# Moving fold steps, one load and one small product between the slots of a hand-scheduled kernel (FFT mixing followed by a low-rank mixer, one core)

## The chip, the cores and the metric

The kernel runs on one core of a Trainium2 chip. A core has TensorE for matmuls (PE in the profile, PEld for its weight loads), VectorE (DVE), ScalarE (ACT), GpSimd (POOL), SyncE (SP), whose queue issues most transfers here, and 16 DMA engines. The metric is the time of one execution on the device, in microseconds; several runs are made and their median is the number that counts.

## The reference

`x` is 8 batches of 3136 rows of 256 channels, float32. Two things are computed one after the other:

```python
X = np.fft.fft(x, axis=1)              # along the 3136 rows
X = np.fft.fft(X, axis=2)              # along the 256 channels
x = X.real.astype(np.float32)

xt = x.transpose(0, 2, 1)
h = xt @ U @ V                         # rank 32 over the rows
u = x + h.transpose(0, 2, 1)
ch = np.maximum(u @ w_ch1, 0.0) @ w_ch2   # 256 -> 1024 -> 256
out = (u + ch).astype(np.float32)
```

## The kernel before

The work has two layers that run interleaved: a transform of each batch (the two Fourier transforms and the low-rank part), and a mixer over chunks of rows that yields the output.

**Transform of a batch b.** Rows of `x` are loaded into one buffer each: `xf` (rows in reversed order, by four gathers on POOL, line 57) and `xr` (rows in order, by two transfers on SP, line 76, and small ones for a single partition, lines 87 to 102). There is one `xf` and one `xr`, so a load of the next batch has to wait until the present batch's part has been read. `load_part` (line 487) loads half a batch. `fold` (line 471) yields the steps that turn them into the operands of the transform, by sums and differences on VectorE, all recorded through `fold_tt` (line 452, so that the profile has them under L453):

- `along_d` (line 416) adds or subtracts mirrored channels: `eof<-xf` and `eor<-xr`; `alone` (line 423) copies the two channels left over, on POOL.
- `mirror` (line 427) makes `eos` out of `eof` and `eor`; `half` and `fourth` make `ge`, `go` and `gc`.

For a batch after the first two the steps come in this order, counted from 0: `eof`, `eof`, `eor`, `eor`, load of the next batch's first half, `eos`, `eos`, `eof`, `eof`, `eor`, `eor`, load of the next batch's second half, `eos`, `eos`, `ge`, the two `gc`, `go`. Batch 1 has its `eor` steps in the part before the loop, and so four steps fewer: its step 7 is the load of batch 2's second half. The last batch loads nothing.

Then `transform` (line 928) gives the matmul steps: `even_rows` and `seq` (tiles `pt`, with `ev` and `eh` copied or made from them), `join` and `mirrored` (sums on VectorE into the tiles `A`, `B` and `tab`), the channel steps `chan` (line 656: two matmuls into `pst`, then a copy into `S` or `T`), `lowrank` (line 670: `ptt`, copied by ScalarE into `tl` and `ta`), and `hidden` (line 740: `pq` from `tl`, copied into `qt`), whose result is spread by a DMA transpose into `qf` (line 750). All PSUM tiles of the transform, and the tiles `ph` of the mixer, share two buffers, named `dft`.

**Mixer over chunks.** The 8 x 1568 rows of half the batches are cut into 25 chunks c of 512; each chunk also gives the mirrored rows of the other half (hf = 1). For each chunk and half, `front` (line 770) makes two small matmuls `ph` and sums them on VectorE with `S` and `T` into `u` (line 799, under L458); a DMA transpose on SP brings `u` into `ut` (line 813), of which POOL makes the small tiles `fx` (lines 816, 817). `odd_part` (line 820) makes `uo = S - T`. `direct` (line 829) multiplies `u` of the first half with W1 (`p<-u,w`), ScalarE applies relu into `h` (line 843); `mirrors` (line 845) corrects the same PSUM tiles to the other half by `uo` and `qf` (`p<-uo,wd`, `p<-dv,qf`), again with relu (line 859). `second_product` (line 890) multiplies `h` with W2 (`p<-w,h`, two PSUM buffers named `p2`), VectorE adds `ut` into the output tile `o` (lines 921, 922), POOL corrects a column by `fx` (line 926), and `store` (line 879) sends `o` out over SP. There are two buffers of `o`.

**Order.** Each chunk of the loop (line 1182) has slots: 0 to 5 and a few fractions between them. `turn(c, sl)` runs what is due in slot 6c + sl. The tuple `FOLDS` (line 1131) and the lists behind it (lines 1137 to 1139, counted from mid - 18, where mid is the batch's first transform slot) say in which slot each fold step of a batch is recorded; `transform` gives its steps from slot mid on. A slot 0 comes right after `direct(c, 0)` and `odd_part(c)`; slot 1 in the middle of a second product; slot 1.75 after `front(c, 1)`; 4.75 after `front(c + 1, 0)`; slot 5 after `second_product(c, 0, 0)`.

What is recorded is not yet the order on an engine: a scheduler places instructions when it thinks them ready. `keep_in_program_order`, which `fold_tt` and `mm` call, holds an instruction behind the one that was recorded just before it on its engine, and behind no other. An instruction without this hold, like `uo`, `u` and `o` in the later chunks or any DMA, can move.

Of the kernel before, what the change touches and what calls it, by code (L numbers as in the profile page):

```python
# [31 lines left out]
def kernel(  # L32
# [9 lines left out]
    nc = tc.nc  # L42
    B, S, D = x.shape
# [418 lines left out]
    def mm(*a, **k):  # L462
        ins = nc.tensor.matmul(*a, **k)  # L463
        if len(pinned) > 1:
            tc.keep_in_program_order(ins)
        if pinned:
            pinned.append(ins)
# [77 lines left out]
    def seq(b, par, typ, pn, tag="dft", part=True):  # L545

        d = state(b)
        ne = NE if b else 0
        pt = psum.tile([P, QW + NE], FP32, tag=tag, name="pt", bufs=BUFS[tag])
        d["pt"] = pt  # L550
        todo = products(b, par, typ, P * typ, pn == 1, ne)
        if typ == 0 and b == 0:
            todo = todo + products(b, par, 1, 256, (pn == 1) == (par == 1), ne)
        elif typ == 0 and pn == 1:
            todo = todo + [(QW, w, rhs) for w, rhs in u_odd(b, 1, 256)]
        add_up(pt, todo)
        if pn == 0:
            ev = d["ev"] = wp.tile([P, QW], FP32, tag="ev", name="ev", bufs=EB)
            w = (2 * NT if par else TE) + ne
            nc.scalar.copy(ev[:, :w], pt[:, :w])  # L560
            if part:
                apart(b, par)
# [12 lines left out]
    def join(b, par, typ, kept=None, low=True, high=True):  # L575

        d = kept or ST[b]
        ne = NE if b else 0
        pt, ev = d["pt"], d["ev"]
        dst = ST[b]["A"] if typ == 1 else ST[b]["B"]  # L580
        p_, e_ = pt[:, 0:2 * NT], d["eh"][:]
        up, dn = dst[:, 1176:784:-1], dst[:, 1177:HALF + 1]
        if low:
            nc.vector.tensor_tensor(up, p_, e_, op=AL.add)
        if not high:
            return
        if typ == 1:
            nc.vector.tensor_tensor(dn, e_, p_, op=AL.subtract)
        else:
            nc.vector.tensor_tensor(dn, p_, e_, op=AL.subtract)  # L590
        if ne:
            pu, eu = 2 * NT, NT
            nc.vector.tensor_tensor(ST[b]["tab"][:, typ, par, :].rearrange("p (g r) -> p g r", r=R),
                                    four(pt[:], pu), four(ev[:], eu), op=AL.add)
            if typ == 0:
                alt = dst[0:1, 786:HALF + 1:2]
                nc.vector.tensor_single_scalar(alt, alt, -1.0, op=AL.mult)
                nc.vector.tensor_copy(ST[b]["tab"][0:1, 0, 1, :].rearrange("p (g r) -> p g r", r=R),  # L598
                                      four(pt[0:1], QW))

    def even_rows(b, typ, pn, tag="dft"):

        d = state(b)
        ne = NE if b else 0
        if pn == 0:
            d["pe"] = psum.tile([P, QW], FP32, tag=tag, name="pt", bufs=BUFS[tag])
        pt = d["pe"]
        todo = products(b, 0, typ, P * typ, pn == 1, ne)
        if typ == 0:
            todo = todo + products(b, 0, 1, 256, pn == 0, ne)  # L610
        for n, (at, w, rhs) in enumerate(todo):
            mm(pt[:, at:at + rhs.shape[-1]], w, rhs, start=(pn == 0 and n == 0),
               stop=(n == len(todo) - 1), skip_group_check=True)
        if pn == 0:
            ev = d["ve"] = wp.tile([P, QW], FP32, tag="ev", name="ev", bufs=EB)
            nc.scalar.copy(ev[:, :TE + ne], pt[:, :TE + ne])  # L616
            return
        dst = d["A"] if typ == 1 else d["B"]
        nc.scalar.copy(strip(dst[:], 392, [[-2, NT + 1]]), pt[:, 0:NT + 1])
        nc.scalar.copy(strip(dst[:], 391, [[-2, NT]]), pt[:, NT + 1 + ne:TE + ne])  # L620
        if ne:
            nc.scalar.copy(d["tab"][:, typ, 0, :].rearrange("p (g r) -> p g r", r=R), four(pt[:], TE - NT))
# [7 lines left out]
    def mirrored(b, typ, kept):  # L630

        ne = NE if b else 0
        pt, ev = kept["pe"], kept["ve"]
        dst = ST[b]["A"] if typ == 1 else ST[b]["B"]
        nc.vector.scalar_tensor_tensor(strip(dst[:], 394, [[-1, 2], [2, NT]]),
                                       strip(ev[:], 1, [[NT + ne, 2], [1, NT]]), 2.0 if typ else -2.0,
                                       strip(pt[:], 1, [[NT + ne, 2], [1, NT]]),
                                       op0=AL.mult, op1=AL.subtract if typ else AL.add)
# [17 lines left out]
    def chan(b, ch, h, tag="dft", eng=None):  # L656
        d = ST[b]
        at, n0 = ((0, 0), (785, 1), (393, 786), (1177, 785))[ch]
        n = 393 if ch == 0 else 392
        if b == 0 and ch == 2:  # L660
            at, n0, n = 392, 784, 393
        pt = psum.tile([P, TE], FP32, tag=tag, name="pst", bufs=BUFS[tag])
        mm(pt[:, :n], MC[:, h * P:(h + 1) * P], d["A"][:, at:at + n], start=True, stop=False)
        mm(pt[:, :n], (MSX if ch == 3 and b == 0 else MSN)[:, h * P:(h + 1) * P], d["B"][:, at:at + n],
           start=False, stop=True)
        to = d["ST"[h]][:, n0:n0 + 2 * n - 1:2]
        eng = eng or (nc.vector.tensor_copy if b == 0 and h == 1 else nc.scalar.copy)
        eng(to, pt[:, :n])  # L668
# [71 lines left out]
    def hidden(b):  # L740

        pt = psum.tile([P, JT, R], FP32, tag="dft", name="pq", bufs=BUFS["dft"])
        for j in range(JT):
            for s in range(2):
                mm(pt[:, j, :], W1[:, s, j * P:(j + 1) * P], TL[:, s, :], start=(s == 0), stop=(s == 1))
        nc.scalar.copy(QT[:], pt[:].rearrange("p j r -> p (j r)"))
        if b > 1:
            spread_rank(b)

    def spread_rank(b):  # L750

        (nc.scalar if b == 1 else nc.sync).dma_start_transpose(out=QF[b % 2][:], in_=QT[:])
# [175 lines left out]
    def transform(b):  # L928

        def odd_rows(typ, pn):  # L930
            seq(b, 1, typ, pn)
            if pn:
                join(b, 1, typ)

        def even(typ, pn):
            even_rows(b, typ, pn)
            if pn:
                mirrored(b, typ, ST[b])

        a = [lambda pn=pn: even(1, pn) for pn in range(2)]  # L940
        s = [lambda pn=pn: even(0, pn) for pn in range(2)]
        c = [lambda pn=pn: odd_rows(1, pn) for pn in range(2)]
        d = [lambda pn=pn: odd_rows(0, pn) for pn in range(2)]
        rank = [lambda: lowrank(b)]
        ch = [lambda ch=ch, h=h: chan(b, ch, h) for ch in range(2) for h in range(2)]
        q = [lambda: hidden(b)]
        if b == 1:
            return 11, [a[:1], c[:1] + a[1:], c[1:] + d[:1], s[:1] + d[1:] + s[1:],
                        [lambda ch=ch: chan(b, ch, 0, eng=nc.vector.tensor_copy) for ch in (1, 0)], [ch[3], ch[1]],
                        rank + q + [lambda: spread_rank(b)]]  # L950
        if b == 2:
            return 23, [a[:1], a[1:] + c[:1], [], c[1:] + s[:1], s[1:], d[:1], d[1:], ch[:1], ch[1:2] + rank,
                        q, ch[2:3], ch[3:]]
        return 6 * (b * HALF // CH) - 15, [[x] for x in a + c + d[:1] + s + d[1:] + ch[:1] + rank + ch[1:2] + q + ch[2:]]
# [173 lines left out]
    def put(slot, *steps):  # L1128
        due.setdefault(slot, []).extend(steps)

    FOLDS = {1: (5, 5, 6, 6, 6, 7, 8, 8, 9, 9, 10, 10, 10.75),
             2: (13, 13.75, 15, 15, 15, 16, 16, 17, 18, 19, 20, 20, 20, 21, 21, 22, 22.75),
             3: (26, 26, 30, 30, 30, 31, 31, 32, 33, 33, 34, 34, 35, 35, 36, 37, 38)}
    for b in range(1, B):
        mid, steps = transform(b)
        todo = list(fold(b))
        places_ = FOLDS.get(b) or [mid - 18 + n for n in
                                   ((1, 2, 3, 5, 5, 5, 5, 8, 9, 10, 11, 11, 12, 13, 14, 15, 17) if b + 1 < B else
                                    (1, 2, 3, 5, 5, 5, 8, 9, 10, 11, 12, 13, 14, 15, 17))]
        assert len(todo) == len(places_)  # L1140
        for step, at in zip(todo, places_):
            put(at, step)
        for n, step in enumerate(steps):
            put(16.5 if mid + n == 17 and b == 1 else mid + n, *step)
# [98 lines left out]
```

## Time and profile before

| | |
|---|---|
| median of 3 runs | 440.24 us (439.96 to 440.59) |
| profiled execution | 440.81 us |
| its span in the profile | 439.0 us |
| granted TensorE clock, mean | 0.998 |
| DMA, mean over the span | 154 GB/s, 67.83 MB |

The profile lists instructions with their start and duration in microseconds from the start of the span; `x16` says that sixteen alike are merged in a row, and `[0.38 <-DVE u L458]` that the engine stood idle for 0.38 us before and what ended this. Tiles are written out<-in by the names above. Most matmuls are recorded by a helper and have L463. An engine with q behind its name (SPq) is its queue of instructions that issue DMAs. The ends of matmuls are modelled, so their starts are the better number. A matmul's record is missing here and there, so that a group of eight can show as x7.

### The profile page before, as it was taken

The numbers are of one execution on the slowest core, as the hardware profiler recorded it, in microseconds if no ns is written. First come the engines' busy times: TensorE is split into PE (matmuls) and PEld (weight loads), VectorE is DVE, ScalarE is ACT, GpSimd is POOL, SyncE is SP. The second block draws the span as 40 slices with busy tenths as digits, with TensorE's granted clock in tenths as the row PEclk, the third lists the DMA queues.
The fourth block names the chain that finished last, engine by engine and source line by source line (L and its number), as shares of the span: only waits on it lengthen the run. The fifth ranks groups of instructions, "written<-read, shape, count | busy, mean of one in ns | idle before, by whom it ended". The sixth has DMA issues, their size and how long they took to land.

```text
span 439.0 us, 9351 instructions
## 1 busy us (share of the span) xinstructions
PE 422.1 (96%) x3457; PEld 284.1 (65%) x3504; DVE 319.9 (73%) x665; ACT 292.2 (67%) x633; POOL 139.8 (32%) x340
## 2 busy tenths in 40 slices
PE   5989998999999999999999999999999999999996
PEld 2764675666666766666666766666666766666675
DVE  8988987987988887769867787679867554353442
ACT  7958764666667757766667757766667757765651
POOL 8971323452333235413343134231422100111111
PEclk9999999999999999999999999999999999999999
DMA  7897798959669685926776386676234423434543
GB/s 200 218 211 197 159 258 123 192 154 244 161 140 246 131 208 140 233 73 178 169 191 193 90 230 72 144 208 142 67 88 132 110 73 95 103 117 124 121 122 122
DMA packets 89165, 67.83 MB, mean 154 GB/s; under 512 B 55402, under 2 KB 82430, under 8 KB 89118
## 3 DMA queue, kind: packets, MB, share of 16 engines
q1 hardware_dynamic: 83350, 52.79, 49.7%
q0 software_dynamic: 5472, 14.36, 12.9%
q8 instruction: 27, 0.44, 0.4%
q14 instruction: 20, 0.16, 0.1%
q10 hardware_dynamic: 296, 0.07, 0.1%
HBM read 28.86 MB, written 25.69 MB: 124 GB/s over the span
## 4 chain that ended last, share of the span: by engine, by line
PE 87%; DVE 4%; ACT 3%; DMA 2%; POOL 2%; issue 1%; POOLq 0%; ACTq 0%
PE p L463 71%; PE pt L463 7%; PE pst L463 5%; PE ph L463 2%; DMA xf<-in_x_dram,xidx 2%; ACT h L843 1%; POOL xf L57 1%; DVE eof L453 1%; PE ptt L463 1%; DVE u L458 1%; PE pq L463 1%; DVE eor L453 1%; DVE eos L453 1%; ACT h L859 0%; POOL em L283 0%
## 5 line engine op out<-in xcount | busy, mean ns | idle before, releaser
L463 PE MATMUL p<-w,h 128*128 128x256 bf16 x1576 | 195.1, 273 | 0.0
L463 PEld LDWEIGHTS <-h 128*128 128x128 bf16 x1576 | 148.7, 98 | 39.8 <-issue 15.3
L859 ACT ACTIVATE h<-p 128x512 bf16<-128x512 f32 (+1 forms) x200 | 101.6, 593 | 82.8 <-PE p L463 79.3
L843 ACT ACTIVATE h<-p 128x512 bf16<-128x512 f32 (+1 forms) x200 | 101.7, 597 | 8.2 <-PE p L463 7.7
L926 POOL TENSOR_TENSOR o<-o,fx 128x2 f32<-128x2 f32 (+1 forms) x95 | 49.0, 516 | 155.4 <-DVE o L922 83.1
L463 PE MATMUL p<-u,w 128*128 128x512 bf16 (+1 forms) x354 | 90.8, 374 | 3.2 <-ACT u L723 0.5
L921 DVE TENSOR_TENSOR o<-p,ut 128x256 f32<-128x256 f32 (+1 forms) x95 | 39.6, 416 | 71.5 <-PE p L463 48.7
L463 PEld LDWEIGHTS <-w 128*128 128x128 bf16 x512 | 41.6, 97 | 38.4 <-issue 2.4
L463 PE MATMUL p<-uo,wd 128*128 128x512 bf16 (+1 forms) x199 | 50.6, 375 | 0.3
L458 DVE TENSOR_TENSOR u<-ph,T 128x512 bf16<-128x512 f32 (+23 forms) x63 | 34.3, 556 | 10.2 <-PE ph L463 8.1
L57 POOL DMA_INDIRECT xf<-in_x_dram,xidx x32 | 36.3, 1135 | 11.0 <-issue 6.8
L922 DVE TENSOR_TENSOR o<-p,ut 128x256 f32<-128x256 f32 (+1 forms) x95 | 38.8, 409 | 0.0
L453 DVE TENSOR_TENSOR eof<-xf 99x1016 bf16<-99x1016 f32 (+1 forms) x33 | 38.4, 1173 | 0.4 <-issue 0.4
L453 DVE TENSOR_TENSOR eor<-xr 99x1016 bf16<-99x1016 f32 (+1 forms) x34 | 38.6, 1146 | 0.0
L458 DVE TENSOR_TENSOR u<-ph,S 128x512 bf16<-128x512 f32 (+23 forms) x63 | 34.2, 554 | 0.8 <-PE ph L463 0.3
L817 POOL TENSOR_TENSOR fx<-ut 128x4 f32<-128x4 bf16 x48 | 17.7, 369 | 53.5 <-DMA ut<-u 53.4
L463 PEld LDWEIGHTS <-wd 128*128 128x128 bf16 x200 | 19.4, 98 | 13.1 <-issue 0.4
L463 PE MATMUL pt<-te,gc 98*128 98x229 bf16 (+1 forms) x192 | 24.0, 260 | 0.2 <-ACT ev L616 0.2
L668 ACT CAST T<-pst 128x392 bf16<-128x392 f32 (+1 forms) x28 | 17.1, 614 | 9.3 <-PE pst L463 9.3
L463 PE MATMUL pst<-A,mc 128*128 128x392 bf16 (+1 forms) x60 | 19.8, 330 | 3.2 <-DVE tab L598 1.6
L463 PEld LDWEIGHTS <-gc 98*128 98x128 bf16 x216 | 19.4, 97 | 4.3 <-issue 0.3
L668 ACT CAST S<-pst 128x392 bf16<-128x392 f32 (+1 forms) x28 | 17.4, 620 | 6.1 <-PE pst L463 6.0
(179 smaller groups left out, 447.3 us busy)
## 6 DMA issues: line engine op xcount, KB each, us to landing
out_dram<-o SPq DMA_DIRECT2D x33, 512.0 KB
xr<-in_x_dram SPq DMA_DIRECT2D x15, 784.0 KB
out_dram<-o SPq DMA_DIRECT2D x8, 384.0 KB
out_dram<-o SPq DMA_DIRECT2D x8, 256.0 KB
out_dram<-o SPq DMA_DIRECT2D x10, 128.0 KB
xr<-in_x_dram SPq DMA_DIRECT2D x2, 392.0 KB
ut<-u SPq DMA_TRANSPOSE x48
vv<-vv SPq DMA_DIRECT2D x3, 196.0 KB
```

Of the source, the lines that this page charges most:

```text
L57: nc.gpsimd.indirect_dma_start(out_, None, bass.AP(t.tensor, t.offset, [[w, rows], [1, w]]), bass.IndirectOffsetOnAxis(idx, 0), element_of ...
L453: ins = nc.vector.tensor_tensor(*a, **k)
L458: ins = nc.vector.tensor_tensor(*a, **k)
L463: ins = nc.tensor.matmul(*a, **k)
L668: eng(to, pt[:, :n])
L817: nc.gpsimd.tensor_tensor(fx[:, :, 1], ut[:, 0:n, 0] if hf else ut[:, n:2 * n, 0], ut[:, n + 1:2 * n + 1, 0], op=AL.subtract)
L843: nc.scalar.activation(k["h", 0][q][:, j - 4 * q, :w], p1[:, :w], AF.Relu)
L859: nc.scalar.activation(k["h", 1][q][:, g, :w], k["p1"][g][:, :w][:, ::-1], AF.Relu)
L921: nc.vector.tensor_tensor(o[:, ts, 0:P], p2[:, :w, 0:P], ut[:rows, ts, 0:P], op=AL.add)
L922: nc.vector.tensor_tensor(o[:, ts, P:D], p2[:, :w, P:D], strip(ut[:rows], (CH // P + t0 + 1) * P, [[P, w], [-1, P]]), op=AL.add)
L926: nc.gpsimd.tensor_tensor(o[:, ts, cols], o[:, ts, cols], fx[:rows, ts, 1 - hf:], op=AL.add)
```

## The change

Three things change, all in the slots in which steps are recorded; no step is added or removed.

```diff
         if b == 1:
             return 11, [a[:1], c[:1] + a[1:], c[1:] + d[:1], s[:1] + d[1:] + s[1:],
-                        [lambda ch=ch: chan(b, ch, 0, eng=nc.vector.tensor_copy) for ch in (1, 0)], [ch[3], ch[1]],
-                        rank + q + [lambda: spread_rank(b)]]
+                        [lambda ch=ch: chan(b, ch, 0, eng=nc.vector.tensor_copy) for ch in (1, 0)], ch[3:] + rank,
+                        ch[1:2] + q + [lambda: spread_rank(b)]]
...
-    FOLDS = {1: (5, 5, 6, 6, 6, 7, 8, 8, 9, 9, 10, 10, 10.75),
-             2: (13, 13.75, 15, 15, 15, 16, 16, 17, 18, 19, 20, 20, 20, 21, 21, 22, 22.75),
-             3: (26, 26, 30, 30, 30, 31, 31, 32, 33, 33, 34, 34, 35, 35, 36, 37, 38)}
+    FOLDS = {1: (5, 5, 6, 6, 6, 7, 8, 12, 9, 9, 10, 10, 10.75),
+             2: (13, 13.75, 15, 15, 15, 16, 16, 16.75, 17, 19.75, 20, 20, 20, 21, 21, 22, 22.75),
+             3: (26, 26, 29, 29, 30, 31, 31, 32, 33, 33, 34, 34, 35, 35, 36, 37, 38)}
...
         places_ = FOLDS.get(b) or [mid - 18 + n for n in
-                                   ((1, 2, 3, 5, 5, 5, 5, 8, 9, 10, 11, 11, 12, 13, 14, 15, 17) if b + 1 < B else
-                                    (1, 2, 3, 5, 5, 5, 8, 9, 10, 11, 12, 13, 14, 15, 17))]
+                                   ((1, 2, 3, 5, 5, 5, 5, 7.75, 8, 10.75, 11, 11, 12, 13, 14, 15, 17) if b + 1 < B else
+                                    (1, 2, 3, 5, 5, 5, 7.75, 8, 10, 11, 12, 13, 14, 15, 17))]
```

For batch 1, `lowrank` is recorded in slot 16 instead of the second of two channel steps, which goes to slot 16.5 (where 17 is due for this batch), in front of `hidden`. Batch 2's second half is loaded in slot 12 instead of 8. For batch 2, step 7 (`eof`) goes from slot 17 to 16.75, step 8 (`eof`) from 18 to 17, step 9 (`eor`) from 19 to 19.75. For batch 3, steps 2 and 3 (`eor`) go from slot 30 to 29. For batches 4 to 6, counted from mid - 18, step 7 (`eof`) goes from 8 to 7.75, step 8 (`eof`) from 9 to 8, step 9 (`eor`) from 10 to 10.75. For batch 7 its two `eof` steps of the second half do the same, and its `eor` steps stay in 10 and 11.

## The prediction

> **What bounds the kernel now.** I read the page first, for the busy times.
>
> ```profile
> span 439.0 us, 9351 instructions
> PE 422.1 (96%) x3457; PEld 284.1 (65%) x3504; DVE 319.9 (73%) x665; ACT 292.2 (67%) x633; POOL 139.8 (32%) x340
> ```
>
> TensorE is busy for 96% of the span. A rearrangement that leaves every matmul in place can therefore gain only what TensorE now waits. The view of waits, for TensorE alone, names the two largest that lie behind the start-up:
>
> ```profile
> PE pst L463 <- DVE tab L598: 1.6, 1, 1.6
> PE pst L463 <- DVE u L458: 1.5, 4, 0.4
> ```
>
> So the stake is a few us. The four waits on `u` repeat once a batch; the other, and some smaller ones, lie between 75 and 85 us. The timeline shows what each consists of.
>
> **Part 1: second halves of the folds, batches 4 to 7.** One of the four waits, and the same place one batch later, where no next batch is folded:
>
> ```profile
> 313.05 1.92 PE L463 MATMUL p<-w,h 128*128 128x256 bf16 x16
> 313.50 1.20 DVE L453 TENSOR_TENSOR eof<-xf 99x1016 bf16<-99x1016 f32 x1
> 314.62 0.67 DVE L458 TENSOR_TENSOR u<-ph,S 128x512 bf16<-128x512 f32 x1
> 315.35 0.33 PE L463 MATMUL pst<-A,mc 128*128 128x393 bf16 x1 [0.38 <-DVE u L458]
> ```
>
> ```profile
> 362.56 1.92 PE L463 MATMUL p<-w,h 128*128 128x256 bf16 x16
> 363.00 0.67 DVE L458 TENSOR_TENSOR u<-ph,S 128x512 bf16<-128x512 f32 x1
> 364.32 0.33 PE L463 MATMUL pst<-A,mc 128*128 128x393 bf16 x1
> ```
>
> `pst` takes a `dft` PSUM buffer that the sum `u` has to empty first. At 313 a fold `eof` of 1.20 us stands before that sum; at 362 none does. From the sixteen second-product matmuls to `pst` it takes 315.35 - 313.05 = 2.30 us with the fold and 364.32 - 362.56 = 1.76 without: 0.54 us a place. The fold got there because it is pinned only behind the instruction recorded just before it on VectorE, which in that slot is the difference `uo`; `uo` needs little and floats to the front, and the fold goes with it. The change puts the two `eof` steps in slots 4.75 and 5, where a `u` or an `o` sum was recorded last. In the built order of the changed kernel both `u` sums then stand ahead of the fold for batches 4, 5 and 6. For batch 7 they do not: its list keeps `eor` in slot 10, the `eof` of slot 9 that stood before it is gone, so now `eor` is pinned behind `uo` and takes the place before the sums. It lasts as long as `eof`, so that wait stays. Gain 3 x 0.54 = 1.62 us; bounds 0, if another wait shows up behind it, and 4 x 0.54 = 2.16. The row of 364.32 is evidence against another wait: there all else is alike and nothing holds `pst`. The folds put later (`eor` in 10.75) run behind the `u` sums of the second half of a chunk, which feed only a transpose. Queued behind that `eor` on VectorE is the `o` sum of the next half, whose PSUM buffer TensorE wants back two second products later. I cost that at nothing; without that cover it would be up to 1.20 us a batch.
>
> **Part 2: batch 1's low-rank product, and batch 2's fold at 17.** Between 79 and 85 us:
>
> ```profile
> 79.23 0.20 PE L463 MATMUL ptt<-tab,mc 128*128 128x32 bf16 x2
> 79.74 0.43 PE L463 MATMUL pq<-tl,w 128*128 128x32 bf16 x11 [0.30 <-ACT tl L682]
> 81.61 1.21 DVE L453 TENSOR_TENSOR eof<-xf 99x1016 bf16<-99x1016 f32 x1
> 81.64 1.92 PE L463 MATMUL p<-w,h 128*128 128x256 bf16 x16
> 83.54 0.39 PE L463 MATMUL p<-u,w 128*128 128x512 bf16 x1
> 84.20 1.67 PE L463 MATMUL p<-u,w 128*128 128x512 bf16 x7 [0.27 <-DVE u L458]
> ```
>
> `hidden` (`pq`) waits for ScalarE to copy `tl` out of the low-rank product that ran just before it: 79.74 instead of about 79.28, 0.46 us. The change runs that product one step earlier, with eight second-product matmuls and a channel step between, 8/16 x 1.76 + 0.33 = 1.2 us of cover against 0.46. Then the first product waits for `u`, again behind an `eof`: due at 81.64 + 1.76 = 83.40, it starts at 83.54, and its second matmul comes 0.66 us later where the pace is (1.67 - 0.39)/6 = 0.21: 0.14 + 0.45 = 0.59 us. With `eof` at 16.75 the sums start about 1.1 us sooner, and this goes. Together 1.05 us.
>
> Not all of it lasts. The `eor` of slot 19 is put behind the `u` sums of chunk 3's second half, and from there VectorE is full up to the next chunk:
>
> ```profile
> 90.65 0.65 DVE L458 TENSOR_TENSOR u<-ph,S 128x479 bf16<-128x479 f32 x1
> 91.66 0.42 DVE L921 TENSOR_TENSOR o<-p,ut 128x256 f32<-128x256 f32 x1 [0.36 <-issue]
> 92.33 1.20 DVE L453 TENSOR_TENSOR eor<-xr 99x1016 bf16<-99x1016 f32 x1
> 97.85 0.41 DVE L458 TENSOR_TENSOR uo<-S,T 128x512 bf16<-128x512 bf16 x1
> 98.18 0.68 DVE L458 TENSOR_TENSOR u<-ph,S 128x512 bf16<-128x512 f32 x1
> 98.78 0.67 DVE L458 TENSOR_TENSOR u<-ph,T 128x512 bf16<-128x512 f32 x1
> 99.31 0.81 PE L463 MATMUL p<-u,w 128*128 128x512 bf16 x3
> ```
>
> Now: sums end at 91.30, two `o` sums from 91.66, `eor` at 92.33, no gap until `u` ends at 99.45, and the second matmul of the first product follows at 99.31 + 0.21 = 99.52. Changed: the sums end 1.05 earlier at 90.25, the moved `eor` takes 1.20 and the two `o` sums 92.33 - 91.66 = 0.67, so the second `eor` starts at 92.12, 0.21 earlier. `uo` of this chunk moves behind `go`, which takes 98.18 - 97.85 = 0.33 out. `u` ends 0.54 earlier and TensorE, 1.05 ahead, waits 0.51. Part 2 is worth 0.54 us; bounds 0.21 (without `uo`) and 1.05.
>
> **Part 3: batch 3's folds from slot 30 to 29.**
>
> ```profile
> 119.27 1.04 PE L463 MATMUL p<-w,h 128*128 128x256 bf16 x8
> 120.29 0.34 PE L463 MATMUL pst<-A,mc 128*128 128x393 bf16 x1
> ```
>
> `pst` waits here for the joins of batch 2 to empty its buffer: due at 119.27 + 8/16 x 1.76 = 120.15, late by 0.14. In the changed order both `eor` of 1.2 us stand behind the joins instead of before, so the joins end up to 1.2 us earlier. Gain 0.14, bounds 0 and 0.14.
>
> **Part 4: loading batch 2's second half in slot 12.** In the built order it moves less than it says. The four gathers of `xf` still follow one another on POOL and the two large loads of `xr` on SP; only the 12 KB and 4 KB loads of line 87 go behind two stores and the transpose `ut` of chunk 2. The transfers issued from 56 to 59 us, and the timeline around them:
>
> ```profile
> out_dram<-o SPq DMA_DIRECT2D x1, 384.0 KB
> out_dram<-o SPq DMA_DIRECT2D x1, 127.0 KB
> ...
> xr<-in_x_dram SPq DMA_DIRECT2D x1, 12.0 KB
> xr<-in_x_dram SPq DMA_DIRECT2D x1, 4.0 KB
> ```
>
> ```profile
> 57.62 0.79 SPq L887 DMA_DIRECT2D out_dram<-o  x2
> 60.24 10.02 SPq L813 DMA_TRANSPOSE ut<-u  x1
> 67.69 1.92 PE L463 MATMUL p<-w,h 128*128 128x256 bf16 x16
> 70.36 0.53 SPq L887 DMA_DIRECT2D out_dram<-o  x1
> 72.99 0.42 DVE L921 TENSOR_TENSOR o<-p,ut 128x256 f32<-128x256 f32 x1 [2.19 <-PE p L463]
> 75.40 0.34 PE L463 MATMUL pst<-A,mc 128*128 128x392 bf16 x1 [1.56 <-DVE tab L598]
> ```
>
> This is the largest wait, 1.56 us at 75.40: the joins run behind an `o` sum that starts only at 72.99. Its matmuls were over by 69.7, so the releaser named is not the one. What it also needs is its `o` buffer, held by the two stores issued at 57.62, 384 and 127 KB. The transpose behind them on the queue, held for 10.02 us, fits a store that drains slowly. The two stores are issued when ScalarE has their data, so they start no earlier; only 16 KB leave from ahead of them. If that speeds them in proportion to size, 16 of 527 KB over 15.4 us, it gives 0.45; bounds 0 and 1.56. I take 0.3. [...]
>
> **Sum.** 1.62 + 0.54 + 0.14 + 0.3 = 2.60 us. The profiled execution took 440.81 us, 439.0 of span and 1.8 around it; it becomes 438.2. It lies 0.57 above the median of the runs, 440.24, so the forecast for the median is 437.6.
>
> **Rivals.** (a) The store chain of part 4 clears by a us or more: 437.6 - 1.2 = 436.4. For: the `o` sum then finds its data ready since 69.7. Against: only 16 KB move.
>
> (b) The gains are given back: with TensorE ahead, other VectorE chains become what it waits for, as at 98.78. If two thirds of part 1 and all of part 2 go, 0.54 + 0.14 + 0.3 = 1.0 us stays, 439.3; if all goes, 440.2. For: VectorE has 73% on average and no gap for 7 us at 92. Against: the 362 row.
>
> (c) Slower. In the changed order of POOL the `fx` of chunk 2 stands ahead of the second `o` addition of chunk 1.
>
> ```profile
> 68.56 0.19 POOL L926 TENSOR_TENSOR o<-o,fx 128x2 f32<-128x2 f32 x1 [0.18 <-DVE o L922]
> 74.08 0.20 POOL L817 TENSOR_TENSOR fx<-ut 128x4 f32<-128x4 bf16 x1 [5.29 <-DMA ut<-u]
> 87.39 1.34 SPq L813 DMA_TRANSPOSE ut<-u  x1
> 89.08 0.41 PE L463 MATMUL p<-dv,qf 32*128 32x32 bf16 x8
> ```
>
> `fx` waits for a transpose until 74.08, so the addition goes from 68.56 to about 74.3, 5.7 us later. Its store, now at 70.36, and the transpose queued behind it on SP follow at about 74.6, into the gathers and loads of 75 to 87 us. Among these is the transpose `qf`, which TensorE needs at 89.2; SP's next transpose, which waits for it, starts at 87.39. If `qf` slips by the full 5.7 us, TensorE stands until 93.0 instead of 89.2, part 2 is lost, and the total is 440.24 + 3.8 - 1.62 - 0.14 = 442.3. It decides from a landing of `qf` past about 91; up to 88.1, where TensorE will want it, it costs nothing. Against: the bytes are the same, and the queue has until 88.1.
>
> **Numbers.** Forecast 437.6 (437.0 to 438.5) 0.60; (a) 0.10; (b) 0.17, of which half under 439.4; (c) 0.09, from 440.3 to 442.3; the rest between. Runs of this kernel can tell 0.2% from no change, 0.88 us. Faster than 439.36: 0.60 + 0.10 + 0.09 + 0.02 = 0.81; same 0.11; slower than 441.12: 0.08. Range 436.4 to 439.4, from (a) to the better half of (b).
>
> **What would show it.** Right: of TensorE's four waits on `u` one is left, near 313; from sixteen matmuls to `pst` 1.76 us in the other three; no wait of `pq` near 79; a new short wait of the first product near 98; the wait at 75 smaller but there. Wrong: three or four waits on `u` left (part 1), the `o` sum near 73 starting by 71.5 (a), TensorE standing at `p<-dv,qf` near 88 (c).

## The result, and the profile after

| | before | changed |
|---|---|---|
| median (lowest to highest; 6 runs each) | 440.18 us (439.85 to 441.19) | 437.74 us (436.9 to 438.6) |
| profiled execution / its span | 440.81 / 439.0 us | 437.52 / 435.7 us |

The ratio is 0.9941, with a 95% interval of 0.9924 to 0.9958: faster by 2.44 us, against 2.60 forecast (437.6). The page of the changed kernel shows TensorE with the same work in a shorter span:

```profile
span 435.7 us, 9397 instructions
PE 423.2 (97%) x3504; PEld 284.1 (65%) x3504; DVE 319.7 (73%) x665; ACT 291.7 (67%) x633; POOL 128.8 (30%) x340
```

The view of waits for TensorE (sum, number, longest, in us). The wait on `tab` and three of the four on `u` ahead of `pst` are gone; a short one of `pt` and one of 0.8 us on `h` are new:

```profile
PE p L463 <- ACT h L859: 0.8, 1, 0.8
...
PE pst L463 <- DVE u L458: 0.4, 1, 0.4
PE pt L463 <- DVE u L458: 0.3, 1, 0.3
```

Part 1 in the timeline (start, duration, engine, line). At 262 both `u` sums stand ahead of `eof`, and `pst` follows the sixteen matmuls at the pace: 262.59 - 260.83 = 1.76. At 312, in batch 7, `eor` stands ahead of the sums and the distance is 312.05 - 309.76 = 2.29:

```profile
260.83 1.92 PE L463 MATMUL p<-w,h 128*128 128x256 bf16 x16
261.28 0.67 DVE L458 TENSOR_TENSOR u<-ph,S 128x512 bf16<-128x512 f32 x1
262.48 1.20 DVE L453 TENSOR_TENSOR eof<-xf 99x1016 bf16<-99x1016 f32 x1
262.59 0.33 PE L463 MATMUL pst<-A,mc 128*128 128x393 bf16 x1
...
309.76 1.92 PE L463 MATMUL p<-w,h 128*128 128x256 bf16 x16
310.20 1.20 DVE L453 TENSOR_TENSOR eor<-xr 99x1016 bf16<-99x1016 f32 x1
311.33 0.67 DVE L458 TENSOR_TENSOR u<-ph,S 128x512 bf16<-128x512 f32 x1
312.05 0.33 PE L463 MATMUL pst<-A,mc 128*128 128x393 bf16 x1 [0.38 <-DVE u L458]
```

The stretch of parts 2 and 4 in the timeline of the changed kernel:

```profile
60.33 7.76 SPq L813 DMA_TRANSPOSE ut<-u  x1
71.06 0.42 DVE L921 TENSOR_TENSOR o<-p,ut 128x256 f32<-128x256 f32 x1 [0.17 <-DMA out_dram<-o]
72.04 1.89 PE L463 MATMUL p<-u,w 128*128 128x512 bf16 x8
72.35 0.20 POOL L817 TENSOR_TENSOR fx<-ut 128x4 f32<-128x4 bf16 x1 [6.06 <-DMA ut<-u]
72.66 0.19 POOL L926 TENSOR_TENSOR o<-o,fx 128x2 f32<-128x2 f32 x1
72.88 0.41 SPq L887 DMA_DIRECT2D out_dram<-o  x1
73.39 1.44 SPq L813 DMA_TRANSPOSE ut<-u  x1
73.77 0.33 PE L463 MATMUL pst<-A,mc 128*128 128x392 bf16 x1
78.15 0.37 ACT L746 CAST qt<-pq 128x256 bf16<-128x256 f32 x1
79.39 1.92 PE L463 MATMUL p<-w,h 128*128 128x256 bf16 x16
80.12 0.20 POOL L816 TENSOR_TENSOR fx<-ut 128x4 f32<-128x4 bf16 x1 [4.27 <-DMA ut<-u]
80.14 1.27 ACTq L752 DMA_TRANSPOSE qf<-qt  x1
81.46 2.06 ACT L859 ACTIVATE h<-p 128x512 bf16<-128x512 f32 x4 [2.93 <-PE p L463]
82.11 1.08 PE L463 MATMUL p<-u,w 128*128 128x512 bf16 x4 [0.79 <-ACT h L859]
87.37 0.41 PE L463 MATMUL p<-dv,qf 32*128 32x32 bf16 x8
```

Two things are to be read here. First, the `o` sum starts at 71.06 instead of 72.99, now with the store named as its releaser, and `pst` comes at the pace, 73.77 - 72.04 = 1.73: the largest wait is gone whole, not by 0.3. Second, the chain of rival (c) did start. GpSimd's `fx` stands ahead of the `o` addition, which goes at 72.66 instead of 68.56; its store and the transpose `ut` follow at 72.88 and 73.39. But what is late behind them is ScalarE. `qt` is ready at 78.52, its transpose `qf` is issued on ScalarE's queue at 80.14, just as the transpose `ut` has landed (GpSimd's `fx` waits for the same landing until 80.12), and behind it in order stands relu. It starts at 81.46, and TensorE, due at 79.39 + 1.76 = 81.15, starts `p<-u,w` at 82.11: 0.96 us late, a wait that the forecast did not have. `qf` itself is in time; TensorE does not stand at 87.37.

Part 2's give-back and part 3, in the same view. 97.54 - 95.35 - 1.76 = 0.43 us is waited for `u` (0.51 forecast); and 118.76 - 117.88 = 0.88, where before it was 120.29 - 119.27 = 1.02, is the 0.14 of part 3:

```profile
95.35 1.92 PE L463 MATMUL p<-w,h 128*128 128x256 bf16 x16
97.54 0.56 PE L463 MATMUL pt<-te,gc 98*128 98x229 bf16 x4 [0.28 <-DVE u L458]
...
117.88 1.04 PE L463 MATMUL p<-w,h 128*128 128x256 bf16 x8
118.76 0.33 PE L463 MATMUL pst<-A,mc 128*128 128x393 bf16 x1
```

So between the two profiles: +1.72 us at 75, +0.46 and +0.60 between 79 and 85, -0.96 at 82, -0.43 at 97.5, +0.14, +1.62, and -0.08 from the start-up (the row of 67.69 is at 67.77): 3.07 of the 3.3 us by which the spans differ; the rest is spread in small amounts. The theory from this: the small loads ahead of the store caused the whole 1.72 us, and ScalarE's queue cost 0.96. The rivals: the wait at 75 comes and goes by itself, or the wait at 82 belongs to the low-rank product.

### The profile page after: what moved, and what is told of

Same layout as the page of the kernel before. It is cut to its first block, busy times and chain, and to the rows that moved or that the text cites. A ratio compares the mean times of both kernels' runs of the same rounds, so it can differ in the third digit from the quotient of the medians.

```text
span 435.7 us, 9397 instructions
## 1 busy us (share of the span) xinstructions
PE 423.2 (97%) x3504; PEld 284.1 (65%) x3504; DVE 319.7 (73%) x665; ACT 291.7 (67%) x633; POOL 128.8 (30%) x340
## 4 chain that ended last, share of the span: by engine, by line
PE 79%; DVE 7%; DMA 7%; POOL 2%; ACT 2%; issue 1%; SPq 0%; ACTq 0%; DVEq 0%; POOLq 0%
PE p L463 65%; PE pt L463 7%; PE pst L463 4%; DMA out_dram<-o 3%; DMA xf<-in_x_dram,xidx 2%; DVE eof L453 2%; PE ph L463 2%; DVE eor L453 2%; DMA ut<-u 2%; POOL xf L57 1%; DVE u L458 1%; ACT h L843 1%; PE ptt L463 1%; DVE eos L453 1%; ACT h L859 1%
## 5 line engine op out<-in xcount | busy, mean ns | idle before, releaser
L463 PE MATMUL p<-u,w 128*128 128x512 bf16 (+1 forms) x400 | 93.1, 375 | 1.3 <-ACT h L859 0.8
L926 POOL TENSOR_TENSOR o<-o,fx 128x2 f32<-128x2 f32 (+1 forms) x95 | 40.6, 428 | 157.2 <-DVE o L922 82.5
L817 POOL TENSOR_TENSOR fx<-ut 128x4 f32<-128x4 bf16 x48 | 16.4, 341 | 55.2 <-DMA ut<-u 55.2
L463 PEld LDWEIGHTS <-go 98*128 98x128 bf16 x216 | 16.3, 97 | 6.7 <-issue 0.7
```

Source lines behind the costliest of these rows:

```text
L817: nc.gpsimd.tensor_tensor(fx[:, :, 1], ut[:, 0:n, 0] if hf else ut[:, n:2 * n, 0], ut[:, n + 1:2 * n + 1, 0], op=AL.subtract)
L926: nc.gpsimd.tensor_tensor(o[:, ts, cols], o[:, ts, cols], fx[:rows, ts, 1 - hf:], op=AL.add)
```

## The experiments

Each median stands against the median of the kernel before in runs made together with it. The ratio is estimated over the single runs and is not the quotient of the two medians; the two differ by up to 0.14%, or 0.6 us.

**One part alone: the load.** Only the slot of batch 2's second half.

```diff
-    FOLDS = {1: (5, 5, 6, 6, 6, 7, 8, 8, 9, 9, 10, 10, 10.75),
+    FOLDS = {1: (5, 5, 6, 6, 6, 7, 8, 12, 9, 9, 10, 10, 10.75),
```

> The kernel before with batch 2's second half loaded in slot 12 and nothing else changed (part 4 alone). Theory: the 12 KB and 4 KB loads, once they no longer stand ahead of the two stores of slot 8, let the 127 KB store end sooner, and the o sum that waited for it (72.99 before) starts by 71.5; TensorE's wait of 1.56 us ahead of pst at 75.40 is gone. The same edit turns the order on GpSimd (fx ahead of the o addition), so the transpose ut of SP is issued about 2.4 us later, ScalarE's queue stands at the transpose qf until that has landed, and behind it TensorE waits at p<-u,w near 82 for 0.3 to 1.0 us. Net 0.6 to 1.3 us below the kernel before, ratio 0.997 to 0.9986. Rival 1, the term as it was forecast: the wait at 75 shrinks by 0.3 us and no new wait, ratio 0.9993. Rival 2, the wait at 75 comes and goes from one execution to the next: it is there in this profile with 1.2 us or more.

Measured: 439.3 against 440.22 us, ratio 0.9992 (0.9977 to 1.0008). No wait at 75, and none on `h` at 82. The order on GpSimd is turned, but without the earlier low-rank product `qt` comes later against the rest, and `qf` is held back only until 79.05. The chain is there; its price does not show, because TensorE is 0.60 us late at this place anyway, for VectorE's `u`. One profile without the wait at 75 can't rule out that it comes and goes by itself, and the runs alone can't tell the gain from none.

**All but the load.** The changed kernel with the load back in slot 8.

```diff
-    FOLDS = {1: (5, 5, 6, 6, 6, 7, 8, 12, 9, 9, 10, 10, 10.75),
+    FOLDS = {1: (5, 5, 6, 6, 6, 7, 8, 8, 9, 9, 10, 10, 10.75),
```

> The changed kernel with batch 2's second half loaded in slot 8 again (parts 1 to 3 alone). Theory: the wait of 1.3 to 1.6 us ahead of pst near 75 is back; ut is issued near 71, ScalarE's queue no longer stands at qf, and the wait of 0.96 us near 82 is gone. Beside the changed kernel it loses 1.6 and gains 1.0: 0.4 to 0.9 us slower than it, some 1.8 to 2.3 us faster than the kernel before, ratio to before 0.995 to 0.996. Rival 1, the term as it was forecast: 0.3 us slower than the changed kernel with the wait near 82 still there (it would then belong to the low-rank product that was moved). Rival 2, chance: the wait at 75 is not back.

Measured: 437.62 against 440.22 us, ratio 0.9938 (0.9923 to 0.9953): not slower than the changed kernel (0.9941), which the theory had asked for. The wait at 75 is back, but with 0.59 us, and `p<-u,w` near 82 is 0.24 late:

```profile
74.94 0.34 PE L463 MATMUL pst<-A,mc 128*128 128x392 bf16 x1 [0.59 <-DVE B L597]
79.89 2.14 ACTq L752 DMA_TRANSPOSE qf<-qt  x1
80.73 1.92 PE L463 MATMUL p<-w,h 128*128 128x256 bf16 x16
82.72 2.06 PE L463 MATMUL p<-u,w 128*128 128x512 bf16 x8
```

In the median, then, moving the load brought nothing that can be seen.

**Part 1 alone.** The lists of batches 4 to 7; all instructions before 150 us are as in the kernel before.

```diff
-           ((1, 2, 3, 5, 5, 5, 5, 8, 9, 10, 11, 11, 12, 13, 14, 15, 17) if b + 1 < B else
-            (1, 2, 3, 5, 5, 5, 8, 9, 10, 11, 12, 13, 14, 15, 17))]
+           ((1, 2, 3, 5, 5, 5, 5, 7.75, 8, 10.75, 11, 11, 12, 13, 14, 15, 17) if b + 1 < B else
+            (1, 2, 3, 5, 5, 5, 7.75, 8, 10, 11, 12, 13, 14, 15, 17))]
```

> The kernel before with the new slots for batches 4 to 7 alone (part 1). Theory: three of TensorE's four waits on u go, the one near 315 stays, nothing takes their place: 1.62 us faster, ratio 0.9963 (0.9955 to 0.9975), and everything up to 200 us as before. Rival, the gains are given back: less than 0.6 us, ratio above 0.9985.

Measured: 438.27 against 440.22 us, ratio 0.9957 (0.9943 to 0.9972); one wait on `u` ahead of `pst` is left, and nothing took the place of the others. From its waits and its timeline:

```profile
PE pst L463 <- DVE u L458: 0.4, 1, 0.4
```

```profile
71.05 0.42 DVE L921 TENSOR_TENSOR o<-p,ut 128x256 f32<-128x256 f32 x1 [0.26 <-DMA out_dram<-o]
...
71.87 1.89 PE L463 MATMUL p<-u,w 128*128 128x512 bf16 x8
73.60 0.33 PE L463 MATMUL pst<-A,mc 128*128 128x392 bf16 x1
```

Part 1 is confirmed. The surprise is at 73.60: in an order that is the kernel before's up to here, with the small loads ahead of the store, the wait of 1.56 us is not there. The theory falls as far as the whole wait is laid to the loads. An `o` sum at 71.05 is also no sign of rival (a): it comes here without the load's move.

**The low-rank product alone.**

```diff
-                        ..., [ch[3], ch[1]],
-                        rank + q + [lambda: spread_rank(b)]]
+                        ..., ch[3:] + rank,
+                        ch[1:2] + q + [lambda: spread_rank(b)]]
```

> The kernel before with batch 1's low-rank product one step earlier and nothing else (half of part 2). Theory: the wait of 0.30 us at pq near 79.7 goes and TensorE runs 0.46 us ahead from there, but eof still stands ahead of the sums u that the first product needs near 83.5, and the wait there grows by what was gained: 0 to 0.3 us faster in the end, ratio 0.9993 to 1.000, within what can be told from no change. Rival: the 0.46 us lasts to the end, ratio 0.999.

Measured: 439.97 against 440.22 us, ratio 0.999 (0.998 to 0.9999). The wait of `pq` is gone, and 0.71 us comes back at `p<-u,w` instead of 0.60, but behind ScalarE, not VectorE:

```profile
79.47 2.62 ACTq L752 DMA_TRANSPOSE qf<-qt  x1
82.13 2.06 ACT L859 ACTIVATE h<-p 128x512 bf16<-128x512 f32 x4 [2.69 <-issue]
```

Here `qf` is issued at 79.47 instead of 80.73 and is held on the queue for 2.62 us instead of 1.28. What holds it isn't shown; in the run without the moved load it was 2.14 us.

**The store split.** The kernel before, with a store over 127 partitions issued as 112 and 15.

```diff
-            nc.sync.dma_start(out=...[D, np_]..., in_=o[p:p + np_, t:t + nt, :])
+            cut = np_ - np_ % 16 if np_ == 127 else np_
+            for p0, n in ((0, cut), (cut, np_ - cut)):
+                if n:
+                    nc.sync.dma_start(out=...[D, n]..., in_=o[p + p0:p + p0 + n, t:t + nt, :])
```

> The kernel before, in which a store over 127 partitions is issued as two, over 112 and 15 partitions; nothing of the change. In the earlier runs DMA moved only about 25 GB/s for 3 to 5 us while the 127 KB store drained, and the o sum waited for its end: TensorE's wait at 75 was 1.56, 0.59, 0 and 0.55 us in four profiles in which the small loads stood ahead, 0 in two in which they stood behind. Theory, the store crawls on few DMA engines and chance sets when it starts: split, the plateau of 25 GB/s ahead of 72 us is gone, SP's transpose behind it is held 2 to 5 us instead of 8 to 10, the wait at 75 is 0, and the median falls by the mean of those four waits, 0.7 us: ratio 0.9985 (0.9965 to 0.9995). Rival, the drain is set by the other transfers of that time: plateau or wait of 0.5 us or more still there.

Measured: 439.96 against 440.14 us, ratio 0.9996 (0.9977 to 1.0015). The wait at 75 is 0, and the hold of the transpose behind the store fell to 2.39 us. In the view of DMA from 62 to 74 us each number is the GB/s in a slice of 0.3 us. The kernel before:

```profile
GB/s 444 239 102 198 259 218 253 239 287 376 300 338 280 246 103 51 24 24 24 24 37 218 214 59 24 24 24 24 24 24 24 24 27 24 24 61 285 345 361 382
```

The changed kernel:

```profile
GB/s 225 437 202 246 362 389 386 352 270 266 96 24 24 59 232 187 50 24 24 24 24 24 24 24 24 24 24 27 20 169 285 27 14 0 0 0 0 0 0 195
```

The kernel before with the store split (its profile lies 4.1 us later from the start-up on):

```profile
GB/s 299 324 236 255 213 74 232 174 65 262 458 256 239 307 188 242 208 205 317 376 408 362 388 281 261 226 198 75 123 291 108 0 0 0 0 0 0 0 0 236
```

For some 5 us, with a burst in between, only 24 GB/s move, a sixteenth of the 380 to 440 that other slices reach, and 127 KB at 24 GB/s take 5.4 us. Split, no such stretch is left, nor in the next four us of that profile, up to 78 us. The whole store crawls on what looks like one DMA engine of the 16: their mean busy share is 0.07, from 70 to 72 us in the kernel before and from 67.2 to 70.2 us in the changed one, and 16 x 0.07 is 1.1 engines, an estimate. Why it crawls isn't shown. In the kernel before the stretch ends near 72.6 us, in the changed one near 70.7, and the `o` sum follows at 72.99 and 71.06. The median shows no gain that can be told from none.

**The last wait on `u`.** The changed kernel with batch 7's first `eor` of the second half later.

```diff
-                                    (1, 2, 3, 5, 5, 5, 7.75, 8, 10, 11, 12, 13, 14, 15, 17))]
+                                    (1, 2, 3, 5, 5, 5, 7.75, 8, 10.75, 11, 12, 13, 14, 15, 17))]
```

> The changed kernel with batch 7's first eor of the second half in slot 10.75 as in batches 4 to 6. Theory: the last of TensorE's four waits on u, at 312, goes for 0.54 us: ratio to before 0.9929, 0.9988 of the changed kernel. Rival, VectorE is full there and another chain takes its place: no wait on u, but less than 0.2 us.

Measured: 437.01 against 440.14 us, ratio 0.9943 (0.9926 to 0.9959). 310.82 - 309.06 = 1.76, so the 0.53 us are gone at their place, but neither the ratio nor its interval separates it from the changed kernel (0.9941):

```profile
309.06 1.92 PE L463 MATMUL p<-w,h 128*128 128x256 bf16 x16
310.82 0.33 PE L463 MATMUL pst<-A,mc 128*128 128x393 bf16 x1
```

Up to 200 us this is the changed kernel's order, and yet `p<-u,w` near 82 is 0.22 us late in it, not 0.96: that wait varies too.

**The transpose off ScalarE's queue.** The changed kernel with `qf` of batch 1 on SP.

```diff
-        (nc.scalar if b == 1 else nc.sync).dma_start_transpose(out=QF[b % 2][:], in_=QT[:])
+        nc.sync.dma_start_transpose(out=QF[b % 2][:], in_=QT[:])
```

> The changed kernel with the transpose qf of batch 1 issued on SP instead of ScalarE; in the built order it stands on SP behind the store of 80.65 and ahead of the transpose of 86.14. Theory, ScalarE's queue is what stood: its relu at 81.46 starts by 80.2, TensorE's wait of 0.96 us ahead of p<-u,w at 82.1 goes, qf lands by 87.4 as before, and 0.5 to 0.96 us of it lasts: ratio to before 0.992 (0.9915 to 0.993). Rival 1: relu had another reason, and the wait stays. Rival 2: qf on SP lands after 88 and TensorE stands at p<-dv,qf.

Measured: 436.88 against 440.14 us, ratio 0.9933 (0.9917 to 0.9948).

```profile
79.47 2.06 ACT L859 ACTIVATE h<-p 128x512 bf16<-128x512 f32 x4 [0.74 <-PE p L463]
80.99 1.68 SPq L752 DMA_TRANSPOSE qf<-qt  x1
81.35 1.89 PE L463 MATMUL p<-u,w 128*128 128x512 bf16 x8
86.45 0.41 PE L463 MATMUL p<-dv,qf 32*128 32x32 bf16 x8
```

Relu starts at 79.47 instead of 81.46, `p<-u,w` at the pace, and `qf`, issued at 80.99 where the changed kernel issued it at 80.14, is still in time at 86.45. ScalarE's queue was the cause: in this profile and the two below with `qf` on SP, TensorE is not late near 82, and in all three of this order with `qf` on ScalarE it is, by 0.96, 0.97 and 0.22 us.

**The low-rank product back.** The changed kernel without that edit (the diff of the run with it alone, reversed).

> The changed kernel with batch 1's low-rank product back in its place ahead of hidden. In the three profiles with the product moved, relu behind the transpose qf started 7.69, 7.14 and 7.61 us after pst near 75; in the three others 6.66, 6.91 and 6.51. Theory, the move brings ScalarE to the transpose while its queue cannot take it and gains nothing: the wait of 0.3 at pq is back (0.46 us), the wait of 0.96 at p<-u,w is 0.3 at most, and the kernel is 0 to 0.5 us faster than the changed one: ratio to before 0.993 to 0.9945. Rival, the move is worth its 0.46 us: 0.46 us slower than the changed one, ratio 0.995.

Measured: 437.78 against 440.14 us, ratio 0.9951 (0.9936 to 0.9965). `pq` waits 0.46 us again, and `p<-u,w` is still 0.49 late, where I had expected 0.3 at most, since `qf` is issued only at 80.40. Together 0.95, the 0.96 us of the changed kernel's profile: next to the turned order on GpSimd the move of the product is worth nothing that can be seen.

**Both repairs, and with the split store.** The diffs of `eor` and `qf`, then those with that of the store.

> The changed kernel with both repairs: batch 7's eor in slot 10.75, and batch 1's transpose qf issued on SP. The two were 0.7 and 0.9 us below the changed kernel one at a time, at places 230 us apart. Theory: they add, 436.1 to 436.5 us, ratio to before 0.9915 (0.990 to 0.993); no wait on u ahead of pst, no wait on h. Rival: the wait on h was a matter of chance, 0.2 us in the run with eor alone, so that qf adds nothing: 437.0, ratio 0.994.

> As the run before it, and the stores over 127 partitions split into 112 and 15. Theory: in the changed kernel the o sum near 71 waits 0 to 0.5 us for the store, and TensorE not at all or 0.1 us, so the split gains 0 to 0.2 us: ratio to before 0.991 to 0.9915. The hold of SP's transpose falls from 7.4 to 8.1 us to 2 to 3 us, the relu behind qf no longer matters. Rival: the store near 72.9 and what follows on SP come sooner and gain 0.5 us or more further on.

Measured: 436.51 and 436.16 against 440.61 us, ratios 0.9904 (0.9875 to 0.9933) and 0.990 (0.9872 to 0.9929). Both medians are below those of the two kernels compared here. In the medians the repairs add: against the kernel before the medians fell by 2.44 us (changed), 3.13 (`eor`), 3.26 (`qf`) and 4.10 (both), where 2.44 + 0.69 + 0.82 is 3.95. The ratios show less: with one repair, 0.9943 and 0.9933, they can't be told from the changed kernel's 0.9941, and with both, 0.9904, the intervals still overlap (0.9875 to 0.9933 beside 0.9924 to 0.9958). The split adds nothing that can be told. In neither profile is TensorE late at 75 or 82.

**Both kernels profiled again.**

> The kernel before, profiled once more. Theory: the wait at 75 is a matter of chance, it is not again 1.56 us but something between 0 and 1.2, and the span is shorter by the difference. Rival: 1.4 to 1.7 us again.

> The changed kernel, profiled once more. Theory: no wait at 75 (0.2 us at most); the wait at p<-u,w near 82, 0.96 us in the first profile and 0.2 us in the run of the same order with eor later, is somewhere between 0 and 1.0 us, the later the transpose ut lands, the longer. Rival: 0.9 to 1.0 us again.

Measured: 440.23 and 439.58 us, one execution each, too few to compare their times. The kernel before, in its second profile:

```profile
72.34 0.42 DVE L921 TENSOR_TENSOR o<-p,ut 128x256 f32<-128x256 f32 x1 [1.10 <-DMA out_dram<-o]
...
74.75 0.34 PE L463 MATMUL pst<-A,mc 128*128 128x392 bf16 x1 [0.49 <-DVE tab L598]
```

The changed kernel, in its second profile:

```profile
73.15 0.42 DVE L921 TENSOR_TENSOR o<-p,ut 128x256 f32<-128x256 f32 x1 [1.93 <-DMA out_dram<-o]
...
75.63 0.34 PE L463 MATMUL pst<-A,mc 128*128 128x392 bf16 x1 [1.36 <-DVE tab L598]
...
82.17 1.28 ACTq L752 DMA_TRANSPOSE qf<-qt  x1
83.50 2.06 ACT L859 ACTIVATE h<-p 128x512 bf16<-128x512 f32 x4 [2.94 <-PE p L463]
84.14 1.08 PE L463 MATMUL p<-u,w 128*128 128x512 bf16 x4 [0.81 <-ACT h L859]
```

The changed kernel can have the wait at 75 after all, nearly as long as the kernel before in its first profile. My expectation of 0.2 us at most was wrong. The table puts the profiles side by side: TensorE's lateness in us, as start less the start of the group of matmuls ahead and its length at the pace (1.73 for eight of the first product, 1.76 for sixteen of the second); the last digit is uncertain by 0.01.

| kernel | `pst` near 75 | `pq` | `p<-u,w` near 82 |
|---|---|---|---|
| small loads ahead of the store: | | | |
| before, first and second profile | 1.72, 0.66 | 0.46, 0.46 | 0.60, 0.59 |
| part 1 alone | 0 | 0.46 | 0.59 |
| low-rank product alone | 0.72 | 0 | 0.71 |
| all but the load | 0.76 | 0 | 0.24 |
| small loads behind the store: | | | |
| changed, first and second profile | 0, 1.53 | 0, 0 | 0.96, 0.97 |
| last `eor` later | 0 | 0 | 0.22 |
| load alone | 0 | 0.46 | 0.60 |
| low-rank product back | 0.11 | 0.46 | 0.49 |
| `qf` on SP, and with `eor` | 0, 0 | 0, 0 | 0, 0 |
| store split: before, and with both repairs | 0, 0 | 0.46, 0 | 0.60, 0 |

At 75 the mean over the five profiles with the loads ahead is 0.77 us, and over the seven with the loads behind and the store whole 0.23. Within each group the spread (0 to 1.72, 0 to 1.53) is larger than the difference. The `o` sum shows the same tendency: counted from the sixteen matmuls ahead of it (67.69 in the kernel before), it starts after 3.45 to 5.30 us with the loads ahead, and after 3.03 to 3.63 with the loads behind, but for the one profile with 5.04. Twelve profiles do not settle it.

## Why the forecast held, point by point

**Part 1** held in place and size: three waits gone, the fourth left in batch 7 where the built order had shown it, 1.62 us, with no new wait (part 1 alone). Its cover for the later `eor` held as well.

**Part 2** is where the forecast's mechanism was incomplete. The 1.05 us between 79 and 85 went as worked out (0.46 + 0.60), and the give-back near 98 was 0.43 for 0.51. What failed is the step that counted all the 1.05 as free: moving the low-rank product brings ScalarE earlier to the transpose on its own queue, and relu stands behind it. That cost 0.96, 0.97 and 0.22 us in the three profiles of this order, 0.72 on average. Not all of it belongs to part 2: with the load left in its place it was 0.24 (one profile), and with the load moved but not the product 0.49. By itself, then, part 2 was worth about 1.06 - 0.24 - 0.43 = 0.39 us, not 0.54; the other 0.48 comes with the load, which makes `ut` late. With `qf` on SP part 2 is 1.06 - 0.43 = 0.63.

**Part 3** measured its 0.14.

**Part 4** was right in what holds the sum: a store that keeps the `o` buffer, named as the sum's releaser for 1.10 and 1.93 us in the second profiles. With the one of 127 KB split the wait is 0 (two profiles). That the small loads ahead of it lengthen the wait is not shown. The size was a guess between bounds (16 of 527 KB over 15.4 us is 0.47, not 0.45): taken at 0.3, in the profiled pair 1.72, but over twelve profiles 0.77 - 0.23 = 0.54 us, with a spread that leaves even the sign open. The pair had caught one of the longest waits of the kernel before and none of the changed kernel. What the forecast put at nothing is the other end of the edit, the late `ut`, with whose landing `qf` leaves ScalarE's queue (80.14 beside 80.12): the 0.48 above. That leaves 0.54 - 0.48 = 0.06, and the medians agree: 437.62 without the load's move, 437.74 with it.

**The rivals.** (a)'s sign shows in the first profile (`o` sum at 71.06, before 71.5) and not in the second (73.15), and it shows with part 1 alone (71.05), so that it was no test of part 4. (b) is at work only at 97.5, as in the forecast. (c) began as written, with the addition, the store and the transpose `ut` 2.4 to 4.1 us late, but not at its price: `qf` kept its margin, and the delay came out on ScalarE's queue, for up to 1 us instead of 3.8. The step that failed in it is that a late transpose costs nothing as long as `qf` lands by 88.1: it looked at `qf`'s landing, and not at what stands behind its issue.

**The sum.** 1.62 + 0.39 + 0.14 + 0.06 = 2.2 us beside 2.44 measured (1.85 to 3.35 by the interval of the ratio), and 2.60 forecast. Part 1, three quarters of that sum, was the part that was sure. Parts 2 and 4 were forecast at 0.84 together, and the profiles give 0.45, an estimate from few of them; that the total still came within 0.2 us is in part luck, since an interval of 1.5 us can't show such a gap.

## What to carry to other kernels

A wait that repeats in every stage with the same length, like the four of 0.54 us here, is a safer gain than one that stands once behind a transfer. The latter may be a matter of chance (here 1.72, 0.66 and 0 us in three profiles of the same order), and one profile of each kernel can both show it where it is rare and hide it where it is common. When an operation is moved earlier, look also at what its result sets off on the queue of its own engine: here relu stood behind a transpose that its engine had to issue first. A store can crawl though its bytes are few: with this one of 127 KB over 127 partitions DMA moved 24 GB/s for some 5 us, and with 112 and 15 partitions no such stretch was left.

## What the runs showed of the hardware

- With a store of 127 KB over 127 partitions DMA moved only 24 GB/s for some 5 us, up to 72.6 us in the kernel before and 70.7 in the changed one, at a mean busy share of 0.07 of the 16 DMA engines; 127 KB at that rate are 5.4 us, an estimate. Issued over 112 and 15 partitions it left no such stretch (two profiles). A transpose queued behind it on SP was held 7.2 to 10.0 us whole, 1.4 and 2.4 us split.
- The same order of instructions gave 1.72, 0.66 and 0 us of lateness behind that store (kernel before, twice, and part 1 alone), and 0 and 1.53 in the changed kernel. In the second profile of the changed kernel the stretch of 24 GB/s runs to about 72.8 us instead of 70.7. What sets its start isn't shown.
- ScalarE's transpose `qf` was issued within 0.02 us of the landing of SP's transpose `ut` in both profiles of the changed kernel and with the load alone (80.14, 82.17 and 79.05, beside 80.12, 82.15 and 79.03 for GpSimd's wait on the same landing). The other way round, in the kernel before, SP's transpose of 87.39 waited 4.6 us for the landing of `qf`. Why the one waits for the other isn't shown. With both on SP's queue the next `ut` was issued at 82.76, right behind `qf` (80.99 + 1.68 = 82.67).
- With the low-rank product moved and the load in its old place, the same transpose was held on ScalarE's queue for 2.62 and 2.14 us (issued at 79.47 and 79.89). In the other nine profiles that have it there it was 1.27 or 1.28 (issued from 78.79 to 82.91). Why stays open.
